# A third value buffer, a body for up to 192 tokens and a table made by GpSimd, in a kernel of sparse attention and routed experts

## The chip, the cores and the metric

The kernel runs on one core of a Trainium2 chip. Its time is the device time of one execution in microseconds (us), as the median of several runs. An execution was also recorded by the hardware profiler; every row below is from that record. The engines are PE (TensorE, matrix products; PEld is its loading of the stationary operand), DVE (VectorE), ACT (ScalarE), POOL (GpSimd) and SP (SyncE, which here issues nearly all loads).

## The reference

Attention over 24 blocks of 32 tokens, of which each block sees its neighbours, the first and last block and three blocks drawn at random; its output goes through a mixture of eight experts, one expert per token:

```python
# q, k, v: 4 batches x 8 heads x 768 tokens x 64
mask = |blk_i - blk_j| <= 1 or blk_i, blk_j in (first, last) or blk_j in sampled_blocks[blk_i]
attn = softmax(where(mask, q k^T / 8, -1e9)) v
x = attn as 3072 tokens x 512
logits = x @ w_gate + modality_bias[modality_id]      # 8 experts
e = argmax(logits);  p = softmax(logits)[e]
out[token] = p * (relu(x @ w1[e]) @ w2[e])            # 512 -> 1024 -> 512
```

Counted from the inputs, three experts get tokens: 1498, 442 and 1132. In groups of 256 that is five whole groups and 218 tokens, one and 186, four and 108.

## The kernel before, in words

**Attention.** The first and last block (which see everything) are worked densely. The other 22 blocks are taken two at a time and two batches at a time: 22 tiles `g` = 0..21, eleven for each half of the batches. A tile's keys lie in one of two `kbuf`, its values in one of two `vbuf`. Its value loads are `fetch_v` (L505, two block loads of 128 KB, L510) and `fetch_own` (L544, six, L549); two further blocks come from the tile before by copies of GpSimd in `share_v` (L527, L532). Products with the shared blocks are `weigh_shared` (L608), with the tile's own blocks `weigh_own` (L617). `turned` (L624) and `gate` (L634) then turn the output and work out the logits, and `put_row` writes the rows to `x_d` (L1316). The order on each engine is written out by hand: a clock of steps `t`, a table of lags, and `side(t, ...)`, which hangs a load on a step. Value loads hang on `last(g - 2)`, the step of the last scores of the tile that had the same buffer. SP issues its queue in program order, so a load that waits for its buffer holds up all behind it.

**Routing.** `finish` (L1175) makes from the counts of tokens per expert two tables. `hoh` (L1212), multiplied on PE (L1243), gives for every place in every group the number of its token (`gi`, L1081). `grp` (L1239) gives each group's expert, and in columns 22 and 23 the number of whole groups and of all. Two groups of full size are picked before all tokens are known (`NEAR` = 2) and worked into the tail of the attention.

**Experts.** A group has 256 tokens (`GT`). `gather` (L770) fetches its rows by an indirect DMA of GpSimd, `turn_blocks` or `turn_low` (L801) turns them. A weight is split into a rounded high part (ACT, L756) and a low rest (DVE, L759; for the four numbers in `POOL_SPLITS` GpSimd), and each product is three: high by high, high by low, low by high. `first_layer` has `up` (L810; L814, L815, L816: 32 times, weights stationary, 256 token columns moving) and `relu` (L818). `second_layer` has `down` (L824; L829, L830, L831: for each of eight feature blocks and both halves of the tokens, 512 columns of weights moving). `give` (L843) scales by `p` and scatters (L850). Groups 2 to 11 run in a loop without conditions; then `later(12)` asks at run time whether there is another group and whether it is a whole one or holds at most 128 tokens, which `half_group` (L1018) works with tokens as the stationary side. With these inputs there are twelve whole groups and one half group.

Of the kernel before, what the change touches and what calls it, by code (L numbers as in the profile page):

```python
# [30 lines left out]
GT = 256  # L31
NG = NTOK // GT
# [45 lines left out]
LATER = 19  # L78
XD = (7, 7)
# [12 lines left out]
def attention_moe(ctx, tc, kD, qD, qH, v0, v1, blocks, modality, w_gate, bias, w1, w2, out):  # L92
# [32 lines left out]
    with ExitStack() as actx:  # L125
# [18 lines left out]
        vbuf = [slot(7 + n)[:, 0:3072].rearrange("p (c f) -> p c f", c=3) for n in range(2)]  # L144
# [360 lines left out]
        def fetch_v(m, half):  # L505
            i, g = 2 * m + 1, half * NM + m
            vg = vbuf[g % 2]

            def rows_in(r, c, j):
                nc.sync.dma_start(vg[r, c, :].rearrange("p (b f) -> p b f", b=HB), vblock(half, j))  # L510

            if m < 2:
                for n, j in ((0, 0), (1, NB - 1)):
                    rows_in(slice(32 + 32 * n, 64 + 32 * n), 1, j)
            if m == 0:
                for n in range(2):
                    rows_in(slice(0, 32), 1 + n, i + 2 * n)
                for n in range(2):
                    rows_in(slice(96, P), n, i - 1 + 2 * n)
                return  # L520
            rows_in(slice(0, 32), 2, i + 2)
            rows_in(slice(96, P), 1, i + 1)
# [4 lines left out]
        def share_v(m, half):  # L527
            g = half * NM + m
            shared.append(g)
            new, old = vbuf[g % 2], vbuf[(g - 1) % 2]  # L530
# [13 lines left out]
        def fetch_own(m, half, n):  # L544
            i, g = 2 * m + 1, half * NM + m
            vg = vbuf[g % 2]
# [56 lines left out]
        def weigh_shared(g, o, a):  # L603
            vg = vbuf[g % 2]
# [6 lines left out]
        def weigh_own(g, o, a):  # L611
            vg = vbuf[g % 2]
# [197 lines left out]
        def up(g, c, f, o):  # L810
            h, l = wh[(8 * g + c) % NRING], wl[(8 * g + c) % NRING]
            o = o[:, (f % 2) * GT:(f % 2 + 1) * GT]
            fs = slice(f * P, (f + 1) * P)
            nc.tensor.matmul(o, lhsT=h[:, fs], rhs=xh[g % 2][:, c, :], start=c == 0 and f % 2 == 0, stop=False)  # L814
            nc.tensor.matmul(o, lhsT=h[:, fs], rhs=xl[g % 2][:, c, :], start=False, stop=False)  # L815
            nc.tensor.matmul(o, lhsT=l[:, fs], rhs=xh[g % 2][:, c, :], start=False, stop=c == 3 and f % 2 == 1)  # L816

        def relu(k, o):  # L818
            rh = hh[0][:, 2 * k:2 * k + 2, :].rearrange("p a b -> p (a b)")
            rl = hl[k // 2][:, k % 2 * 2:k % 2 * 2 + 2, :].rearrange("p a b -> p (a b)")  # L820
# [3 lines left out]
        def down(g, f, t, o):  # L824
# [6 lines left out]
            nc.tensor.matmul(o, lhsT=hl[f // 4][:, f % 4, ts_], rhs=h[:, fs], start=False, stop=f == 7)  # L831

# [10 lines left out]
        def give(g, t, o):  # L843
# [3 lines left out]
            else:  # L847
                nc.vector.tensor_scalar(og[t], o, w, None, ALU.mult)
            ix = si_e[g] if g < NEAR else si[:, 2 * g:2 * g + 2]
# [131 lines left out]
        def first_layer(g):  # L981
            for c in range(4):
                ahead(8 * g + c)
                if c == 0 and g + 1 < NGMAX:
                    if g == NEAR:
                        gather(g + 1)
                    if g == NG - 1:
# [4 lines left out]
                for f in range(8):  # L992
                    up(g, c, f, hp[f // 2])
            for k in range(4):
                relu(k, hp[k])

        def second_layer(g):
            for k in range(4):
                ahead(8 * g + 4 + k)
                for f in (2 * k, 2 * k + 1):  # L1000
                    for t in range(2):
                        down(g, f, t, op[t])
                if k == 1 and g + 1 < NGMAX:
# [3 lines left out]
            for t in range(2):  # L1007
                give(g, t, op[t])

# [8 lines left out]
        def half_group(g):  # L1018
# [34 lines left out]
            split(8 * g + 6, nc.gpsimd)  # L1053
# [120 lines left out]

        def finish():  # L1175
# [3 lines left out]
            nc.vector.tensor_tensor(gcount2, cnt, narrow, ALU.add)  # L1179
            yield  # L1180
# [3 lines left out]
            nc.vector.tensor_scalar(gwide, gcount2, 8, None, ALU.logical_shift_right)  # L1184
            yield
            gh = small.tile([P, E], F32, name="gh", bufs=1)
            nc.vector.tensor_tensor(gh, gnum, gwide, ALU.subtract)
            yield
            nc.vector.scalar_tensor_tensor(gh, gh, 16.0, iota_f[:, 0:E], ALU.mult, ALU.add)
# [5 lines left out]
            nc.vector.tensor_tensor(start[:, :, 0:E], before_e, gnum.unsqueeze(1).broadcast_to([P, E, E]), ALU.mult)  # L1195
            yield
            gbase = small.tile([P, E], F32, name="gbase", bufs=1)
# [3 lines left out]
            nc.vector.tensor_reduce(gfrom, start[:, :, 0:E], axis=AX.X, op=ALU.add)  # L1201
            hb = small.tile([P, NT, E], F32, name="hb", bufs=1)
# [6 lines left out]
            nc.vector.scalar_tensor_tensor(hc, hs, 2.0, rhi, ALU.mult, ALU.add)  # L1209
            yield  # L1210
# [4 lines left out]
            gend = small.tile([P, E], F32, name="gend", bufs=1)  # L1215
            nc.vector.tensor_scalar(gfrom, gfrom, float(NEAR), None, ALU.add)
            yield
            nc.vector.tensor_tensor(gend, gfrom, gnum, ALU.add)
            ge = work.tile([P, 512], F32, name="y", bufs=3)[:, 0:24 * E].rearrange("p (t e) -> p t e", e=E)
            gl = work.tile([P, 512], F32, name="y", bufs=3)[:, 0:24 * E].rearrange("p (t e) -> p t e", e=E)  # L1220
            i24 = iota_f[:, 0:24].unsqueeze(2).broadcast_to([P, 24, E])
            nc.vector.tensor_tensor(ge, gfrom.unsqueeze(1).broadcast_to([P, 24, E]), i24, ALU.is_le)
            yield
            nc.vector.tensor_tensor(gl, gend.unsqueeze(1).broadcast_to([P, 24, E]), i24, ALU.is_gt)
            yield
            nc.vector.tensor_tensor(ge, ge, gl, ALU.mult)
            yield
            nc.vector.tensor_tensor(ge, ge, iota_f[:, 0:E].unsqueeze(1).broadcast_to([P, 24, E]), ALU.mult)
            yield
            nc.vector.tensor_reduce(grp_f, ge, axis=AX.X, op=ALU.add)  # L1230
            nc.vector.tensor_reduce(grp_f[:, 23:24], gend, axis=AX.X, op=ALU.max)
            gw = small.tile([P, 1], F32, name="gw", bufs=1)
            nc.vector.tensor_reduce(gw, gh, axis=AX.X, op=ALU.max)
            yield
            nc.vector.tensor_scalar(gw, gw, 16.0, None, ALU.is_ge)
            yield
            nc.vector.tensor_tensor(grp_f[:, 22:23], grp_f[:, 23:24], gw, ALU.subtract)
            yield
            nc.vector.tensor_copy(grp, grp_f)  # L1239
# [98 lines left out]
        for g in range(2 * NM):  # L1338
# [11 lines left out]
            vt = last(g - 2) + VL[0]  # L1350
# [6 lines left out]
            for n in range(2):  # L1357
                side(last(g - 2) + VG[n][0], vg[n], VG[n][1])
# [110 lines left out]
        LOOP = MAN - {ET.PE}  # L1469
        with tc.manual_schedule(engines=LOOP):  # L1470
            for g in range(NEAR, NG):
                first_layer(g)
                second_layer(g)
        total = nc.values_load(grp[0:1, 23:24], min_val=NG, max_val=NGMAX, skip_runtime_bounds_check_because=NO_CHECK)
        wide = nc.values_load(grp[0:1, 22:23], min_val=NG - 1, max_val=NGMAX, skip_runtime_bounds_check_because=NO_CHECK)

        def later(g):
            if g == NGMAX:
                return
            with tc.If(total > g):  # L1480
                experts.clear()
                with tc.If(wide <= g) as less:
                    half_group(g)
                with less.Else():
                    experts.clear()
                    with tc.manual_schedule(engines=LOOP):
                        first_layer(g)
                        second_layer(g)
                    later(g + 1)

        later(NG)
# [36 lines left out]
```

## Time and profile before

| | us |
|---|---|
| median of three runs | 521.59 |
| the three runs | 517.51, 521.59, 521.68 |
| the profiled execution | 523.39 |
| its span, first to last instruction | 521.7 |
| mean granted clock of TensorE | 0.991 of full speed |
| busy: PE, PEld, DVE, ACT, POOL | 500.2, 422.4, 373.3, 335.4, 246.0 |

Busy time is summed over the whole span; the stages have different limits. Attention with the first two expert groups runs to about 252 us, the loop of groups to 502.4, the half group and the last stores to the end. The granted clock is a share of full speed: 1.00 is 2.4 GHz, 0.50 is 1.2 GHz.

### The profile page before, as it was taken

What the parts mean: (1) busy time and instruction counts of PE and PEld (TensorE: products, weight loads), DVE (VectorE), ACT (ScalarE), POOL (GpSimd) and SP (SyncE); (2) the same over time, 40 slices, a digit from 0 to 9 for tenths busy, and PEclk for the clock granted to TensorE, in tenths of its full rate; (3) what the DMA queues carried; (4) which work ended last, traced back from release to release, by engine and by line L of the source; (5) the groups of instructions that cost most, each with busy time, mean ns of one, the idle gap of its engine ahead of it and who ended that gap; (6) DMA issues with size and microseconds to landing.
All of it is one profiled execution on the core that took longest, in us unless ns stands there. A gap on an engine that the chain in (4) does not pass through costs nothing.

```text
span 521.7 us, 18917 instructions
## 1 busy us (share of the span) xinstructions
PE 500.2 (96%) x7124; PEld 422.4 (81%) x7124; DVE 373.3 (72%) x1069; ACT 335.4 (64%) x765; POOL 246.0 (47%) x517
## 2 busy tenths in 40 slices
PE   7999999979999998799999999999999999999994
PEld 5678677757878786698989798998989899898974
DVE  6886577676787888467985867667686766768572
ACT  4799887978879897544445655555564545655561
POOL 6788685566568882323175042322325222342422
PEclk9999999999999999989999999999999999999999
DMA  8977898798667769847788797879678686877950
GB/s 299 317 214 205 243 266 244 207 257 247 202 187 194 220 203 257 248 133 253 230 291 299 248 288 257 281 213 297 199 248 283 221 296 202 283 219 258 287 181 24
DMA packets 65143, 123.84 MB, mean 237 GB/s; under 512 B 9745, under 2 KB 17682, under 8 KB 65042
## 3 DMA queue, kind: packets, MB, share of 16 engines
q1 hardware_dynamic: 60784, 108.88, 68.7%
q0 software_dynamic: 4256, 13.65, 7.4%
q8 instruction: 58, 0.95, 0.8%
q14 instruction: 43, 0.35, 0.3%
q10 hardware_dynamic: 2, 0.00, 0.0%
HBM read 105.97 MB, written 12.86 MB: 228 GB/s over the span
## 4 chain that ended last, share of the span: by engine, by line
PE 77%; DMA 11%; DVE 5%; ACT 2%; issue 2%; SPq 1%; POOL 0%; ACTq 0%; POOLq 0%; DVEq 0%
PE bank L586 8%; PE bank L561 8%; PE bank L814 7%; PE bank L815 7%; PE bank L816 7%; PE bank L831 6%; PE bank L830 6%; PE bank L829 6%; DMA slot<-x_d,gi 5%; PE bank L608 4%; PE bank L617 4%; DMA slot<-w 3%; PE bank L634 3%; PE bank L448 2%; PE bank L430 2%
## 5 line engine op out<-in xcount | busy, mean ns | idle before, releaser
L759 DVE TENSOR_TENSOR slot<-slot 128x1024 fp32r<-128x1024 f32 x99 | 124.8, 1273 | 66.4 <-ACT slot L756 59.6
L756 ACT CAST slot<-slot 128x1024 fp32r<-128x1024 f32 x104 | 107.2, 1047 | 73.2 <-PE bank L815 47.8
L814 PE MATMUL bank<-slot 128*128 128x256 f32 x384 | 108.5, 283 | 0.0
L816 PE MATMUL bank<-slot 128*128 128x256 f32 x384 | 107.8, 281 | 0.0
L815 PE MATMUL bank<-slot 128*128 128x256 f32 x384 | 107.6, 280 | 0.0
L577 ACT ACTIVATE a<-y,mn 128x256 f32<-128x256 f32 x176 | 88.6, 510 | 5.5 <-DVE mn L569 5.5
L850 POOL DMA_INDIRECT out<-slot,si x20 | 27.3, 1363 | 104.5 <-ACT slot L846 101.4
L831 PE MATMUL bank<-slot 128*128 128x512 f32 x192 | 75.9, 396 | 0.5 <-DVE slot L822 0.5
L830 PE MATMUL bank<-slot 128*128 128x512 f32 x192 | 76.0, 396 | 0.0
L829 PE MATMUL bank<-slot 128*128 128x512 f32 x192 | 75.8, 395 | 0.0
L814 PEld LDWEIGHTS bank<-slot 128*128 128x128 f32 x384 | 72.4, 188 | 0.7 <-issue 0.2
L815 PEld LDWEIGHTS bank<-slot 128*128 128x128 f32 x384 | 72.2, 188 | 0.4
L816 PEld LDWEIGHTS bank<-slot 128*128 128x128 f32 x384 | 72.2, 188 | 0.0
L569 DVE CUSTOM_DVE_ANT_1 y<-bank,smask 128x256 f32<-128x256 f32 x176 | 66.2, 416 | 0.4 <-PE bank L561 0.2
L498 POOL COPY slot<-slot 128x128 f32 x264 | 63.5, 293 | 0.0
L591 ACT COPY at<-bank 128x512 f32<-128x512 f32 x88 | 50.6, 576 | 10.3 <-PE bank L586 10.1
L532 POOL TENSOR_SCALAR slot<-slot 32x1024 f32<-32x1024 f32 x40 | 41.6, 1040 | 32.4 <-DMA slot<-v 11.2
L586 PE MATMUL bank<-ident,a 128*128 128x128 f32 x352 | 52.0, 280 | 3.1 <-DVE lhs L387 2.7
L561 PE MATMUL bank<-slot,q_raw 64*32 64x256 f32 x1408 | 48.6, 382 | 0.3 <-issue 0.3
L586 PEld LDWEIGHTS bank<-ident,a 128*128 128x128 f32 x352 | 38.1, 141 | 7.1 <-issue 2.8
L831 PEld LDWEIGHTS bank<-slot 128*128 128x128 f32 x192 | 36.1, 188 | 9.5 <-DVE slot L822 0.9
L830 PEld LDWEIGHTS bank<-slot 128*128 128x128 f32 x192 | 36.0, 188 | 8.2 <-DVE slot L759 0.3
(302 smaller groups left out, 846.4 us busy)
## 6 DMA issues: line engine op xcount, KB each, us to landing
slot<-w SPq DMA_DIRECT2D x100, 512.0 KB
slot<-v SPq DMA_DIRECT2D x188, 128.0 KB
x_d<-xr SPq DMA_DIRECT2D x22, 256.5 KB
q_raw<-qH SPq DMA_DIRECT2D x22, 256.0 KB
slot<-slot SPq DMA_DIRECT2D x120, 32.0 KB
slot<-kD SPq DMA_DIRECT2D x13, 256.0 KB
slot<-v SPq DMA_DIRECT2D x4, 768.0 KB
slot<-v SPq DMA_DIRECT2D x12, 256.0 KB
```

The costliest lines, as they stand in the source:

```text
L561: nc.tensor.matmul(sp[u][32 * pr:32 * pr + 32, b * 256:(b + 1) * 256], lhsT=q[r, b * NPAIR + pr, n, :], rhs=kv[r, s0:s0 + 8, b, pr, :], st ...
L569: nc.vector.tensor_tensor_reduce(y[:, u, :].rearrange("p (s f) -> p s f", s=8), sp[u][:, b * 256:(b + 1) * 256].rearrange("p (s f) -> p s ...
L577: nc.scalar.activation(a[:, u, :], y[:, u, :], AF.Exp, bias=mn[:, u:u + 1], scale=-1.0, accum_out=total[:, u:u + 1])
L586: nc.tensor.transpose(tp[:, k:k + P], a[:, u, c * P:(c + 1) * P], ident)
L756: nc.scalar.copy(h, s)
L759: (eng or (nc.gpsimd if n in POOL_SPLITS else nc.vector)).tensor_tensor(l, s, h.bitcast(F32), ALU.subtract)
L814: nc.tensor.matmul(o, lhsT=h[:, fs], rhs=xh[g % 2][:, c, :], start=c == 0 and f % 2 == 0, stop=False)
L815: nc.tensor.matmul(o, lhsT=h[:, fs], rhs=xl[g % 2][:, c, :], start=False, stop=False)
L816: nc.tensor.matmul(o, lhsT=l[:, fs], rhs=xh[g % 2][:, c, :], start=False, stop=c == 3 and f % 2 == 1)
L829: nc.tensor.matmul(o, lhsT=hh[0][:, f, ts_], rhs=h[:, fs], start=f == 0, stop=False)
L830: nc.tensor.matmul(o, lhsT=hh[0][:, f, ts_], rhs=l[:, fs], start=False, stop=False)
L831: nc.tensor.matmul(o, lhsT=hl[f // 4][:, f % 4, ts_], rhs=h[:, fs], start=False, stop=f == 7)
```

## The change: what it does

1. **Values.** From tile 13 on there are three value buffers; the third lies in `slot(0)`. The value loads of these tiles hang on `last(g - 3)`, one tile sooner. Tile 13, the first in the new buffer, also loads the first and last block into it (two block loads more).
2. **A body for up to 192 tokens**, `group(g, False)`. `up` moves 192 columns. The first 128 tokens go through `down` as before; the remaining 64 through `down_both`, in which the stationary operand holds the high part of 64 tokens beside their low part, so that a feature block takes two matmuls and not three. `give_both` adds the two halves. It stands at group 11, and behind it the half group.
3. **Order and table.** `finish` puts one expert's rest of at most 192 tokens, then one of at most 128, behind the whole groups. `grp` is now made by GpSimd (33 rows of its queue); `hc`, from which `gi` comes, takes three more DVE operations, one of which reads `by` from GpSimd.
4. The half group's third split goes from GpSimd to DVE. The loop without conditions ends one group sooner, and its drain with it.

```diff
+        def vb(g):
+            if g < THIRD_FROM:                                   # 13
+                return vbuf[g % 2]
+            if len(vbuf) == 2:
+                vbuf.append(values_in(0))
+            return vbuf[(2, THIRD_FROM % 2, 1 - THIRD_FROM % 2)[(g - THIRD_FROM) % 3]]
...
-            if m < 2:
+            if m < 2 or g == THIRD_FROM:
                 for n, j in ((0, 0), (1, NB - 1)):
                     rows_in(slice(32 + 32 * n, 64 + 32 * n), 1, j)
...
-            vt = last(g - 2) + VL[0]
+            free = last(g - (3 if g >= THIRD_FROM else 2))
+            vt = free + VL[0]
...
-                side(last(g - 2) + VG[n][0], vg[n], VG[n][1])
+                side(free + VG[n][0], vg[n], VG[n][1])
...
+            nc.tensor.matmul(o, lhsT=h[:, fs], rhs=xh[g % 2][:, c, 0:n], start=c == 0 and f % 2 == 0, stop=False)
+            nc.tensor.matmul(o, lhsT=h[:, fs], rhs=xl[g % 2][:, c, 0:n], start=False, stop=False)
+            nc.tensor.matmul(o, lhsT=l[:, fs], rhs=xh[g % 2][:, c, 0:n], start=False, stop=c == 3 and f % 2 == 1)
...
+                nc.scalar.activation(rh, o, AF.Relu)
+                for r, to in ((slice(0, P), rl[:, :, 0:P]), (slice(P, n), hh[0][:, 2 * k:2 * k + 2, n:GT])):
+                    nc.vector.scalar_tensor_tensor(to, o[:, :, r], 0.0, rh[:, :, r].bitcast(F32), ALU.max, ALU.subtract)
...
+        def down_both(g, f, o):
+            h, l = wh[(8 * g + 4 + f // 2) % NRING], wl[(8 * g + 4 + f // 2) % NRING]
+            fs = slice((f % 2) * 512, (f % 2 + 1) * 512)
+            high = lambda: nc.tensor.matmul(o, lhsT=hh[0][:, f, P:GT], rhs=h[:, fs], start=f == 0, stop=f == 7)
+            low = lambda: nc.tensor.matmul(o[0:64], lhsT=hh[0][:, f, P:THREE], rhs=l[:, fs], start=False, stop=False)
+            for product in (high, low) if f < 4 else (low, high):
+                product()
+
+        def give_both(g, o):
+            nc.vector.tensor_copy(og[1][0:64], o[64:128])
+            nc.vector.tensor_tensor(og[1][0:64], o[0:64], og[1][0:64], ALU.add)
+            nc.vector.tensor_scalar(og[1][0:64], og[1][0:64], share[0:64, 2 * (g % 2) + 1:2 * (g % 2) + 2], None, ALU.mult)
+            scatter(g, 1)
...
-            split(8 * g + 6, nc.gpsimd)
+            split(8 * g + 6)
...
+            nc.vector.tensor_tensor(start[:, :, 0:E], before_e, inner.unsqueeze(1).broadcast_to([P, E, E]), ALU.mult)
...
+            nc.gpsimd.tensor_tensor(whole_n, inner, part[:, 0, :], ALU.add)
...
+            nc.gpsimd.tensor_scalar(by[:, 0:1], move[:, 0, 0:1], 2.0, float(2 * NEAR - 1), ALU.mult, ALU.add)
+            nc.gpsimd.tensor_scalar(by[:, 1:2], move[:, 1, 0:1], 2.0, 0.0, ALU.mult, ALU.add)
...
+            gp.tensor_copy(grp[:, 0:20], grp_f[:, 0:20])
+            gp.tensor_copy(grp[:, 21:24], grp_f[:, 21:24])
...
+            nc.vector.tensor_scalar(hs, rhi, by[:, 0:1], by[:, 1:2], ALU.is_ge, ALU.mult)
+            nc.vector.scalar_tensor_tensor(hs, code_of, pick[:, 0:1], hs, ALU.is_equal, ALU.mult)
+            nc.vector.tensor_tensor(hc, hc, hs, ALU.add)
...
-            nc.vector.tensor_tensor(ge, gfrom.unsqueeze(1).broadcast_to([P, 24, E]), i24, ALU.is_le)
...
-            nc.vector.tensor_copy(grp, grp_f)
...
-            for g in range(NEAR, NG):
+            for g in range(NEAR, NG - 1):
                 first_layer(g)
                 second_layer(g)
...
+        def whole(g):
+            with tc.If(narrower <= g) as less:
+                group(g, False)
+                if g + 1 < NGMAX:
+                    with tc.If(total > g + 1):
+                        half(g + 1)
+            with less.Else():
+                group(g)
+                later(g + 1)
```

SP's queue at the end of the attention; `slot<-v` are value loads, `slot<-w` weights, `x_d<-xr` rows written. Before, from the write of tile 19's rows on:

```order
L1316 DMA x_d<-xr 128x513
L510 DMA slot<-v 32x2x512 x2
L549 ISA
L549 DMA slot<-v 32x2x512
L549 ISA
L549 DMA slot<-v 32x2x512
...
L549 ISA
L549 DMA slot<-v 32x2x512
L745 ISA
L745 DMA slot<-w 128x512
L1316 DMA x_d<-xr 128x513
```

With the change, from the same write on:

```order
L1399 DMA x_d<-xr 128x513
L756 ISA
L756 DMA slot<-w 128x512
L1399 DMA x_d<-xr 128x513
L756 ISA
L756 DMA slot<-w 128x512
```

The eight value loads of the last tile have gone from here to one write of rows earlier; the weights follow the write directly.

GpSimd's queue at the end of the routing; `out<-slot,si_e` are scatters of the first early group, `slot<-x_d,gi` the gathers of groups 2 and 3. Before:

```order
L387 TENSOR_SCALAR lhs<-iota_f,rlo,code 128x128 x2
L759 TENSOR_TENSOR slot<-slot 128x1024
L850 DMA out<-slot,si_e_84 3072x512 x2
L770 DMA slot<-x_d,gi 128x513 x4
L759 TENSOR_TENSOR slot<-slot 128x1024 x2
```

With the change:

```order
L770 TENSOR_TENSOR slot<-slot 128x1024
L1256 TENSOR_TENSOR whole_n<-inner,part 128x8
...
L1276 TENSOR_TENSOR y<-iota_f,ends 128x192 x2
L1278 TENSOR_SCALAR y<-y 128x384
...
L1296 TENSOR_TENSOR grp_f<-y,gx 128x20
L1297 CAST grp<-grp_f 128x20
L1298 CAST grp<-grp_f 128x3
L886 DMA out<-slot,si_e_84 3072x512 x2
L781 DMA slot<-x_d,gi 128x513 x4
L770 TENSOR_TENSOR slot<-slot 128x1024 x2
```

All 33 rows of the table stand between the split and the scatters, and so ahead of the gathers.

DVE's queue in the half group, before (`L759` is a weight's low part, `L1037` the low part of the hidden values that PE multiplies next):

```order
L1022 TENSOR_SCALAR si_half<-si 128x1 x2
L759 TENSOR_TENSOR slot<-slot 128x1024 x2
L1037 TENSOR_TENSOR slot<-bank,slot 128x4x128
L759 TENSOR_TENSOR slot<-slot 128x1024
L1037 TENSOR_TENSOR slot<-bank,slot 128x4x128
```

With the change:

```order
L1062 TENSOR_SCALAR si_half<-si 128x1 x2
L770 TENSOR_TENSOR slot<-slot 128x1024 x3
L1077 TENSOR_TENSOR slot<-bank,slot 128x4x128
L770 TENSOR_TENSOR slot<-slot 128x1024
L1077 TENSOR_TENSOR slot<-bank,slot 128x4x128
```

One more low part of a weight stands ahead of the first low part of the hidden values.

## Rows read from the trace of the kernel before

**Rows 1.** Stretches: length; busy PE, PEld, DVE, ACT, POOL; clock, DMA share, GB/s.

```profile
150.00:180.00 30.00, 30.00 (x852) 23.63 (x846) 23.19 (x117) 27.24 (x91) 23.58 (x68) 1.00 0.72 203
...
217.20:219.90 2.70, 0.06 (x3) 0.00 (x0) 0.00 (x0) 0.00 (x0) 0.00 (x0) 0.86 0.96 352
219.90:226.00 6.10, 6.08 (x102) 5.47 (x102) 3.14 (x10) 3.61 (x6) 0.00 (x0) 0.50 0.27 99
...
480.00:502.40 22.40, 22.40 (x145) 20.34 (x144) 15.77 (x19) 12.21 (x16) 7.35 (x8) 1.00 0.80 249
```

**Rows 2.** Chain of waits at the attention's end: start, us, what.

```profile
209.13 0.94 PE bank L586 x8
...
217.26 2.65 issue
```

**Rows 3.** SP's timeline there: start, us until issued, line, transfer, count.

```profile
210.79 3.43 SPq L549 DMA_DIRECT2D slot<-v  x6
```

**Rows 4.** PE's timeline: the bounds of one group's two layers.

```profile
434.98 0.28 PE L814 MATMUL bank<-slot 128*128 128x256 f32 x1
...
446.25 0.40 PE L829 MATMUL bank<-slot 128*128 128x512 f32 x1
...
457.39 0.28 PE L814 MATMUL bank<-slot 128*128 128x256 f32 x1
```

**Rows 5.** Weight loads by form: count, busy us, mean ns, idle before.

```profile
L814 PEld LDWEIGHTS bank<-slot 128*128 128x128 f32 x384 | 72.4, 188 | 0.7 <-issue 0.2
...
L617 PEld LDWEIGHTS bank<-slot,at 128*32 128x32 f32 x1408 | 22.1, 113 | 0.5 <-issue 0.3
```

**Rows 6.** DVE's timeline in the half group, in brackets the idle time before.

```profile
507.05 1.23 DVE L759 TENSOR_TENSOR slot<-slot 128x1024 fp32r<-128x1024 f32 x1 [1.68 <-PE bank L1033]
508.49 0.69 DVE L1037 TENSOR_TENSOR slot<-bank,slot 128x512 fp32r<-128x512 f32 x1 [0.21 <-ACT slot L1036]
```

**Rows 7.** GpSimd operations by form, from the start of the program.

```profile
L292 POOL TENSOR_SCALAR t<-t 128x24 f32<-128x24 f32 x3 | 1.0, 319 | 0.3
...
L288 POOL TENSOR_TENSOR t<-rb 128x24 f32<-128x24 f32 x3 | 0.7, 233 | 0.2
...
L280 POOL TENSOR_TENSOR rm<-rm,t 128x72 f32<-128x72 f32 x1 | 0.3, 336 | 0.1
```

**Rows 8.** DVE's timeline at the end of the routing.

```profile
245.62 2.33 DVE L1187 TENSOR_TENSOR gh<-gnum,gwide 128x8 f32<-128x8 int32 x1
...
250.08 0.22 DVE L1195 TENSOR_TENSOR start<-before_e,gnum 128x64 f32<-128x64 f32 x1
...
252.79 1.22 DVE L759 TENSOR_TENSOR slot<-slot 128x1024 fp32r<-128x1024 f32 x1
...
257.80 4.63 DVE L759 TENSOR_TENSOR slot<-slot 128x1024 fp32r<-128x1024 f32 x4
```

**Rows 9.** GpSimd's timeline at the end of the routing.

```profile
245.54 2.39 POOL L759 TENSOR_TENSOR slot<-slot 128x1024 fp32r<-128x1024 f32 x1
254.17 1.09 POOL L850 DMA_INDIRECT out<-slot,si_e  x1 [6.24 <-DVE gfrom L1216]
...
263.32 1.73 POOL L770 DMA_INDIRECT slot<-x_d,gi  x1 [6.09 <-DMA slot<-w]
265.35 0.97 POOL L770 DMA_INDIRECT slot<-x_d,gi  x1 [0.30 <-issue]
```

**Rows 10.** The gathers from 262 to 276, us from issue to landing.

```profile
DMA to landing us min/median/max: 6.8/7.4/7.5
```

**Rows 11.** PE's timeline, first turn of group 2's rows.

```profile
272.96 0.60 PE L801 MATMUL bank<-ident,slot 128*128 128x128 f32 x4
```

**Rows 12.** Copies of GpSimd in the loop: ns least, median, most of all 40.

```profile
L779 POOL COPY slot<-slot x40: 387/393/1485, 283.1 to 489.2; 32x256 f32<-32x256 f32 x40
```

**Rows 13.** GpSimd's timeline, three of these copies in one row.

```profile
331.24 2.35 POOL L779 COPY slot<-slot 32x256 f32<-32x256 f32 x3 [4.92 <-DMA out<-slot,si]
```

**Rows 14.** DVE's timeline at the same time.

```profile
332.11 1.22 DVE L759 TENSOR_TENSOR slot<-slot 128x1024 fp32r<-128x1024 f32 x1 [1.66 <-ACT slot L756]
```

More of the change, by code (lines that the diff above doesn't have):

```diff
@@ L31 @@
 GT = 256
+THREE = 192
 NG = NTOK // GT
@@ L78 @@
 LATER = 19
+THIRD_FROM = 13
 XD = (7, 7)
@@ L529, in share_v @@
             shared.append(g)
-            new, old = vbuf[g % 2], vbuf[(g - 1) % 2]
+            new, old = vb(g), vb(g - 1)
             for r, c in ((slice(96, P), 0), (slice(0, 32), 1)):
@@ L992, in first_layer, with second_layer @@
                 for f in range(8):
-                    up(g, c, f, hp[f // 2])
+                    up(g, c, f, hp[f // 2], GT if wide_ else THREE)
             for k in range(4):
-                relu(k, hp[k])
-        def second_layer(g):
+                relu(k, hp[k], GT if wide_ else THREE)
+        def second_layer(g, wide_=True):
             for k in range(4):
@@ L1000, in second_layer @@
                 for f in (2 * k, 2 * k + 1):
-                    for t in range(2):
+                    for t in range(2 if wide_ else 1):
                         down(g, f, t, op[t])
+                    if not wide_:
+                        down_both(g, f, op[1])
                 if k == 1 and g + 1 < NGMAX:
@@ L1006, in second_layer @@
                         gather(g + 2)
-            for t in range(2):
+            for t in range(2 if wide_ else 1):
                 give(g, t, op[t])
+            if not wide_:
+                give_both(g, op[1])
         def down_part(g, f, n, o):
@@ L1173, in choose, with folded @@
                 yield
+        def folded(ap):
+            for n in (4, 2, 1):
+                nc.gpsimd.tensor_tensor(ap[:, :, 0:n], ap[:, :, 0:n], ap[:, :, n:2 * n], ALU.add)
         def finish():
@@ L1179, in finish @@
             nc.vector.tensor_tensor(gcount2, cnt, narrow, ALU.add)
+            gcount3 = small.tile([P, E], I32, name="gcount3", bufs=1)
+            nc.vector.tensor_scalar(gcount3, gcount2, -64.0, None, ALU.add)
             yield
@@ L1469, in attention_moe, with group, half @@
         LOOP = MAN - {ET.PE}
+        def group(g, wide_=True):
+            experts.clear()
+            with tc.manual_schedule(engines=LOOP):
+                first_layer(g, wide_)
+                second_layer(g, wide_)
+        def half(g):
+            experts.clear()
+            half_group(g)
         with tc.manual_schedule(engines=LOOP):
-            for g in range(NEAR, NG):
+            for g in range(NEAR, NG - 1):
                 first_layer(g)
                 second_layer(g)
-        total = nc.values_load(grp[0:1, 23:24], min_val=NG, max_val=NGMAX, skip_runtime_bounds_check_because=NO_CHECK)
-        wide = nc.values_load(grp[0:1, 22:23], min_val=NG - 1, max_val=NGMAX, skip_runtime_bounds_check_because=NO_CHECK)
+        load = lambda n, least, most: nc.values_load(grp[0:1, n:n + 1], min_val=least, max_val=most, skip_runtime_bounds_check_because=NO_CHECK)
+        total, wide, narrower = load(23, NG, NGMAX), load(22, NG - 1, NGMAX), load(21, NG - 1, NGMAX + 64)
+        def whole(g):
[7 more added lines that the diff above has]
+                later(g + 1)
         def later(g):
@@ L1480, in later @@
             with tc.If(total > g):
-                experts.clear()
                 with tc.If(wide <= g) as less:
-                    half_group(g)
+                    half(g)
                 with less.Else():
[L1485 to L1491, printed above, removed]
+                    whole(g)
+        whole(NG - 1)
 _SHAPE_OUT = (NTOK, HD)
```

103 lines of the change are left out of this document (69 added, 34 removed).

## The prediction, made before the changed kernel was run

> **What bounds the kernel now.** I read the table of busy time first: PE is busy for 500 of 521.7 us, so an edit counts where PE works less or waits less. Then the stretches [rows 1]: in the middle of the attention PE is busy 30.00 of 30 us and in the loop of groups 22.40 of 22.4, both at the 2.4 GHz level (clock 1.00). There, moving other engines' work changes nothing. Two stretches differ. From 217.2 to 219.9 PE is busy 0.06 of 2.70 us, no other engine works, and the DMA share is 0.96 with 352 GB/s. From 219.9 to 226.0 PE is busy again but at clock 0.50, the 1.2 GHz level. The chain of waits puts the gap down to issue, 2.65 us, in the middle of a run of matmuls [rows 2]: no instruction of another engine is named as its releaser. Last I read the timelines: SP's for the transfers ahead of the gap, PE's for the pitch of its matmuls, DVE's and GpSimd's for the end of the routing.
>
> The profiled execution took 523.39 us, 1.8 over the median of 521.59; one run of the three took 517.51. The sum below stands against 523.39.
>
> **Part 1, the values.** From tile 13 on, nine tiles' loads of eight transfers (128 KB each) are issued one tile sooner, and two transfers are added at tile 13; on SP they pass the writes of rows and the loads of `q`, which are issued behind them now. In the middle that costs nothing: PE is covered there, 30.00 of 30 [rows 1]. If that cover were gone, the two added transfers would cost what two of the six at the end take to issue, 2/6 of 3.43 = 1.1 us [rows 3]. At the end, the last tile's eight transfers (1 MB) go from just ahead of the gap. The last was issued by 214.22 [rows 3], three microseconds before PE stopped, and with the weights behind them they keep the DMA at 0.96 through the gap [rows 1]. I take the gap to be PE's own instructions coming late behind this traffic, since nothing else released it. With a megabyte less it probably goes. Worth: 2.64 us idle and, at half clock, half of 6.10 = 3.05: **-5.7**. Ends: 0 if the weights, issued sooner now, fill the DMA as much, and -5.7.
>
> **Part 2, the body for 192 tokens.** It takes the place of one of twelve whole groups: the counts 218, 186 and 108 put exactly one rest at 186.
> Down: a whole group has 48 matmuls between 446.25 and 457.39, 0.232 each [rows 4]. The new body has 8 x 3 + 8 x 2 = 40: 8 x 0.232 = **-1.9**.
> Up: 96 matmuls between 434.98 and 446.25, 0.1174 each for 256 columns [rows 4]. With 192 columns they take 0.088 if the columns decide, which would be -2.8. But each also loads 128 columns of weights. Loads of 128 columns take 188 ns and of 32 columns 113 ns [rows 5], 0.78 ns a column, so 0.100 for 128. The transposes, 128 columns loaded for 128 moved, go at 0.94 / 8 = 0.1175 [rows 2]. That bounds the gain from the other side at nothing. I take 0.105, beside the load's slope: 96 x 0.0125 = **-1.2** (ends -2.8 and 0).
> The Trainium skill speaks against the width here: "TensorE: Matmul & The Clock Gate", section "LDWEIGHTS (loading the stationary operand)", gives a weight load its columns over 1.2 in ns, 107 for 128, whatever moves. By it the term would be -1.0, by the columns alone -2.8; the trace's slope is nearer to the page.
> The relu's low part becomes two narrower DVE operations per block and `give_both` three of 64 rows; DVE is busy 15.77 of 22.40 in such a stretch [rows 1], so PE hides them. The three values read for the branch stand on PE's queue where two stood; the branch of before shows no gap in front of the half group, so 0 to one late fetch of instructions, 2.65 as in [rows 2]; I take 0. The drain and the shorter loop: 0, GpSimd is busy 7.35 of 22.40 [rows 1].
>
> **Part 3, the half group.** The third split now runs on DVE ahead of the first low part of the hidden values. DVE ends the second split at 508.28 and the low part starts at 508.49 [rows 6]; with one more split of 1.23 between, it starts at 509.5, and PE, which multiplies it next, waits **+0.9** (0 to 1.0).
>
> **Part 4, the table by GpSimd.** DVE loses thirteen operations and gains some eleven small ones: about even. GpSimd gains 34 operations in a chain. Sixteen narrow ones with two inputs and two casts at 0.233, nine with a scalar at 0.319; by the step from 24 to 72 columns, 0.103 for 48 [rows 7], four of 192 columns at 0.59, two folds at 0.39 and 0.28, and one of 384 at about 1.1. That is 11.2; with 0.07 between two (0.2 idle before three [rows 7]) 13.6, less somewhat, as most are narrower than the priced ones: 13. It starts when DVE has `inner`, as at 250.08 now or a little before [rows 8], say 249.7, and ends at 262.7. Behind it in the queue stand two scatters (1.09 each with the pause [rows 9], 2.2) and then the gathers of group 2: 264.9 in place of 263.32 [rows 9]. The second gather of the group was issued at 265.35 and landed 7.4 later [rows 10], at 272.75; PE turned these rows at 272.96 [rows 11]. The slack is 0.2, so PE would wait 1.4. One DVE operation of this chain waits for `by`, the ninth of the 34; behind it stand the places of the tokens and four splits, with what the removed operations free as room.
>
> But GpSimd does not run freely beside DVE. A copy that takes 0.393 took up to 1.485 [rows 12]: three of them took 2.35 [rows 13] while DVE subtracted a weight's low part from 332.11 for 1.22 [rows 14]. The other way round, a DVE operation on 8 columns took 2.33 [rows 8] while GpSimd's split of 2.39 ran [rows 9]. Where both have two inputs in memory, one waits for the whole of the other. In the chain's 13 us DVE has one such split at 252.79 and four at 257.80 [rows 8], of which at least four fall in: 4 x 1.16 = 4.6. The gathers come at 269.5, 6.2 later than now, and PE waits 6.0. After a wait of 2.65 the clock cost 3.05 more [rows 1]; here 0 to 3.05, I take 1.5. Together **+7.5**. Ends: 1.4 and 12.5 (below). SP reads the table before it loads group 2's weights, which PE needs after the turn; they come late in the shadow of the same wait.
> The Trainium skill has this as a lock in "SBUF — State Buffer", section "Who interferes with whom": whoever of the two starts first holds a shared pair of ports for its whole instruction. The trace agrees (1.485 for 0.393); by the rule without exception the whole exclusion below holds, an estimate of 528.0.
>
> **The sum.** 523.4 - 5.7 - 1.9 - 1.2 + 0.9 + 7.5 = **523.0**. The median of before is 521.6: within 1%, which is 5.2 us and about what a measurement of this kernel can tell from no change.
>
> **The rivals.**
> *The chain stays hidden* (0.25). GpSimd slips its short operations in between DVE's; PE waits 1.4 and keeps its clock: 523.0 - 6.1 = 516.9, and 515.3 with `up` at the columns' rate. For it: most of the 34 are short, and DVE has small operations between its splits. Against: every long collision in the trace made the other wait.
> *Whole exclusion, slower* (0.18). Each two-input operation of DVE holds GpSimd up and each of GpSimd's holds DVE up: beside four splits a fifth, the 912-column compare and the short ones, about 8 us in place of 4.6. Then the table is ready near 270.7, the gathers go at 272.9 and PE waits 9.4, with 3.05 of half clock 12.5, 5.0 more than my term: 528.0. It decides once the gathers are issued later than about 268, from where the wait eats what parts 1 and 2 give.
> *The gap at 217 stays* (0.16). The weights are issued sooner and fill the DMA in the same way. Against the median then: 521.6 - 1.9 - 1.2 + 0.9 + 7.5 = 526.9; with the chain hidden 520.8.
> *Narrow matmuls are slow* (0.06). No matmul of this rounded type with under 256 columns is in the trace. At the transposes' time per column, 0.1175 / 128 = 0.92 ns, 192 take 0.176: 96 x (0.176 - 0.105) = +6.8: 529.8.
> *The new body is not taken* (0.02): parts 2's -3.1 falls away, 526.1.
>
> **How the numbers follow.** My forecast has 0.28, other mishaps and gains 0.05. The likeliest case's own range is 520.5 to 526, by the ends of the clock's and up's terms. Under 516.4 lie half of the hidden chain and a little of the rest: faster by over 1% 0.20. Over 526.8 lie most of the whole exclusion, half of the case in which the gap stays, and the slow matmuls: 0.27. The rest, 0.53, is within 1%. For eight in ten the range reaches into the hidden chain and to the whole exclusion: 515.5 to 529.
>
> **What would show it.** Up's rows of 192 columns: a pitch of 0.105, or 0.088, or 0.176. 16 rows of `down_both` at 0.232. Between 216 and 226 no gap of PE and a clock of 1.00. GpSimd's 33 rows from 249.7: operations far longer than 0.23 to 0.32 beside DVE's splits, the end of the casts, the issue of the first gather (264.9, 269.5 or 272.9), and PE's idle time in front of the first turn of group 2. In the half group PE's wait for the hidden values' low part. The forecast is wrong if the gathers go before 265 or after 272, or if the gap at 217 is still there.

## The result: slower by 1.4%, and the profile after

| | before | with the change |
|---|---|---|
| median of six runs, us | 520.72 | 527.58 |
| the runs | 517.51 to 523.39 | 526.99 to 529.59 |
| ratio, 95% interval | 1 | 1.0138 (1.0105 to 1.0172) |
| span of the profiled execution | 521.7 | 525.1 |

Where the time went, from the starts of the same matmuls in PE's two timelines (us):

| piece of the program | before | after | difference |
|---|---|---|---|
| start to the first matmul of group 1 | 252.43 | 249.35 | -3.1 |
| group 1 to group 2 | 24.19 | 33.27 | **+9.1** |
| group 2 to group 3 | 23.30 | 22.52 | -0.8 |
| group 3 to the group that has the new body | 180.03 | 179.93 | -0.1 |
| that group (256 columns before, 192 after) | 22.49 | 20.01 | **-2.5** |
| half group, first to last matmul | 12.44 | 13.52 | **+1.1** |
| last matmul to the end | 6.8 | 6.5 | -0.3 |

Groups are counted from 0. The first two end at 276.6 in the kernel before, not at 252 as its description has it; at 252 the second of them begins.

The page: PE is as busy as before, GpSimd 19 us more, with 33 instructions more.

```profile
PE 500.1 (95%) x7116; PEld 420.5 (80%) x7116; DVE 376.0 (72%) x1075; ACT 334.6 (64%) x765; POOL 265.2 (51%) x550
```

**The table.** GpSimd's timeline at the end of the routing, against [rows 9]:

```profile
247.41 0.20 POOL L1256 TENSOR_TENSOR whole_n<-inner,part 128x8 f32<-128x8 f32 x1 [2.51 <-DVE si_e L1150]
...
255.22 1.92 POOL L1217 TENSOR_TENSOR y<-y 128x96 f32<-128x96 f32 x3
257.09 1.17 POOL L1284 TENSOR_SCALAR all_n<-inner 128x8 f32<-128x8 f32 x1
258.35 2.45 POOL L1217 TENSOR_TENSOR all_n<-all_n 128x4 f32<-128x4 f32 x3
260.76 1.30 POOL L1287 TENSOR_SCALAR has<-pick 128x2 f32<-128x2 f32 x1
262.14 0.19 POOL L1288 TENSOR_SCALAR has<-has 128x1 f32<-128x1 f32 x1
...
264.60 0.21 POOL L1298 CAST grp<-grp_f 128x3 int32<-128x3 f32 x1
265.29 1.12 POOL L886 DMA_INDIRECT out<-slot,si_e  x1 [0.48 <-ACT slot L767]
...
268.00 1.01 POOL L781 DMA_INDIRECT slot<-x_d,gi  x1 [0.30 <-issue]
```

The chain runs from 247.41 to 264.81, 17.4 us. An operation on a single column takes 0.19 at 262.14; one on eight columns takes 0.20 at 247.41; between 257 and 262 operations on eight and on two columns take 1.17 and 1.30. What ran on DVE then, against [rows 8]:

```profile
252.32 1.52 DVE L770 TENSOR_TENSOR slot<-slot 128x1024 fp32r<-128x1024 f32 x1
...
255.73 4.75 DVE L770 TENSOR_TENSOR slot<-slot 128x1024 fp32r<-128x1024 f32 x4
...
260.62 0.20 DVE L1121 TENSOR_TENSOR gi<-bank,to 128x38 int32<-128x38 f32 x1
260.73 1.22 DVE L770 TENSOR_TENSOR slot<-slot 128x1024 fp32r<-128x1024 f32 x1
```

The four splits from 255.73 on take 4.75, against 4.63 without the chain: DVE loses a tenth of a us on them, and GpSimd gets about one operation in between two splits. DVE is held up too: the split at 252.32 takes 1.52 in place of 1.22, beside GpSimd's operation on 384 columns (2.47, from 251.30), and three new operations for `hc` stand ahead of it; PE waits 1.25 for it in group 1. The tokens' places (`gi`) are there at 260.8. In the kernel before the first gather followed them by 0.3 us, at 263.32:

```profile
262.85 0.20 DVE L1081 TENSOR_TENSOR gi<-bank,to 128x38 int32<-128x38 f32 x1
```

Now the gathers stand behind the chain and go at 268.0. PE's timeline, against [rows 11], and the clock around it (columns as in [rows 1]):

```profile
253.90 0.39 PE L827 MATMUL bank<-slot 128*128 128x256 f32 x1 [1.25 <-DVE slot L770]
...
271.17 0.40 PE L850 MATMUL bank<-slot 128*128 128x512 f32 x1
276.00 0.47 PE L812 MATMUL bank<-ident,slot 128*128 128x128 f32 x1 [4.43 <-DMA slot<-x_d,gi]
276.97 0.90 PE L812 MATMUL bank<-ident,slot 128*128 128x128 f32 x3 [0.51 <-DMA slot<-x_d,gi]
...
278.95 0.63 PE L848 MATMUL bank<-slot 128*128 128x512 f32 x1
```

```profile
271.20:277.00 5.80, 0.87 (x4) 0.21 (x2) 3.44 (x1) 1.04 (x1) 5.47 (x4) 0.79 1.01 401
277.00:281.30 4.30, 4.30 (x14) 3.61 (x15) 3.53 (x4) 1.53 (x2) 0.50 (x1) 0.50 0.83 283
```

PE waits 4.9 us for the gathers, and then works 4.3 us at the 1.2 GHz level, which costs half of them, 2.15. With the 1.25 in group 1 this makes 8.3 of the 9.1.

**The gap at 217** is down to 0.50 us, and the stretch 219.90 to 226.00 now has clock 1.00. What is left stands at the same place of the program: the last tile has 32 products with the shared blocks, and PE stops among them, before the change after the 15th:

```profile
219.91 1.13 PE L608 MATMUL bank<-slot,at 128*64 128x64 f32 x17 [2.65 <-issue]
```

With the change it stops after the 17th:

```profile
218.76 0.68 PE L619 MATMUL bank<-slot,at 128*64 128x64 f32 x15 [0.50 <-issue]
```

```profile
219.90:226.00 6.10, 5.93 (x122) 5.32 (x120) 5.08 (x15) 3.56 (x6) 0.00 (x0) 1.00 0.34 101
```

PE has a longer gap in the attention, 55 us sooner, and the clock of the 15 us after it is 0.89:

```profile
164.38 1.04 PE L619 MATMUL bank<-slot,at 128*64 128x64 f32 x29 [1.39 <-issue]
```

**The new body.** Its first matmul, its first `down` and the half group's first, against [rows 4]:

```profile
485.07 0.25 PE L825 MATMUL bank<-slot 128*128 128x192 f32 x1
...
495.76 0.41 PE L848 MATMUL bank<-slot 128*128 128x512 f32 x1
...
505.08 0.39 PE L1067 MATMUL bank<-slot 128*128 128x512 f32 x1
```

Up: 10.69 / 96 = 0.111 a matmul, against 0.117 with 256 columns. Down: 9.32 / 40 = 0.233, as before, eight fewer.

**The half group** on DVE, against [rows 6]:

```profile
507.05 0.69 DVE L861 COPY slot<-bank 64x512 f32<-64x512 f32 x1
507.78 0.68 DVE L862 TENSOR_TENSOR slot<-bank,slot 64x512 f32<-64x512 f32 x1
508.50 0.48 DVE L863 TENSOR_SCALAR slot<-slot,share 64x512 f32<-64x512 f32 x1
508.90 0.20 DVE L1062 TENSOR_SCALAR si_half<-si 128x1 int32<-128x1 int32 x2
509.02 3.48 DVE L770 TENSOR_TENSOR slot<-slot 128x1024 fp32r<-128x1024 f32 x3
512.43 0.68 DVE L1077 TENSOR_TENSOR slot<-bank,slot 128x512 fp32r<-128x512 f32 x1
```

Not only the third split stands ahead of the hidden values' low part. The three operations of `give_both` hold DVE until 508.98, so that the first split starts 3.9 us after the half group's first matmul; before, it started 1.7 after it. PE waits 0.71 us there for ACT's relu, in front of two transposes that now stand sooner in its queue, and 0.17 for DVE's low part; before the change it had no wait in the half group:

```profile
512.55 0.44 PE L1073 MATMUL bank<-ident,slot 128*128 128x128 f32 x2 [0.71 <-ACT slot L1092]
513.16 0.51 PE L1056 MATMUL bank<-slot 128*128 128x256 f32 x2 [0.17 <-DVE slot L1077]
```

### The profile page after: what moved, and what is told of

Its sections match the earlier page's. It is cut to its first block, busy times and chain, and to the rows that moved or that the text cites. A ratio compares the mean times of both kernels' runs of the same rounds, so it can differ in the third digit from the quotient of the medians.

```text
span 525.1 us, 18946 instructions
## 1 busy us (share of the span) xinstructions
PE 500.1 (95%) x7116; PEld 420.5 (80%) x7116; DVE 376.0 (72%) x1075; ACT 334.6 (64%) x765; POOL 265.2 (51%) x550
## 4 chain that ended last, share of the span: by engine, by line
PE 34%; DMA 11%; DVE 3%; SPq 3%; issue 3%; POOL 1%; ACT 1%; POOLq 0%; DVEq 0%
DMA out<-slot,si 7%; PE bank L825 6%; PE bank L827 6%; PE bank L826 6%; PE bank L850 5%; PE bank L849 5%; PE bank L848 5%; DMA slot<-x_d,gi 3%; SPq L792 2%; DMA slot<-slot 1%; DVE slot L770 1%; DMA slot<-w 1%; POOL slot L781 1%; DVE gmost L1232 0%; SPq L759 0%
## 5 line engine op out<-in xcount | busy, mean ns | idle before, releaser
L827 PE MATMUL bank<-slot 128*128 128x256 f32 (+1 forms) x384 | 107.8, 281 | 1.4 <-DVE slot L770 1.4
L825 PE MATMUL bank<-slot 128*128 128x256 f32 (+1 forms) x384 | 108.3, 282 | 0.0
L826 PE MATMUL bank<-slot 128*128 128x256 f32 (+1 forms) x384 | 107.6, 280 | 0.0
L886 POOL DMA_INDIRECT out<-slot,si x20 | 29.4, 1472 | 96.8 <-ACT slot L879 82.8
L827 PEld LDWEIGHTS bank<-slot 128*128 128x128 f32 x384 | 72.4, 188 | 1.8 <-DVE slot L770 1.8
L848 PE MATMUL bank<-slot 128*128 128x512 f32 x184 | 73.4, 399 | 0.0
L849 PE MATMUL bank<-slot 128*128 128x512 f32 x184 | 73.3, 398 | 0.0
L850 PE MATMUL bank<-slot 128*128 128x512 f32 x184 | 73.2, 398 | 0.0
L825 PEld LDWEIGHTS bank<-slot 128*128 128x128 f32 x384 | 72.4, 189 | 0.6
L826 PEld LDWEIGHTS bank<-slot 128*128 128x128 f32 x384 | 72.3, 188 | 0.4
L597 PE MATMUL bank<-ident,a 128*128 128x128 f32 x352 | 53.1, 283 | 1.1 <-ACT a L431 0.5
L790 POOL COPY slot<-slot 32x256 f32<-32x256 f32 x40 | 19.6, 490 | 46.5 <-DMA out<-slot,si 34.7
L850 PEld LDWEIGHTS bank<-slot 128*128 128x128 f32 x184 | 34.9, 190 | 8.3 <-DVE slot L841 0.2
```

The costliest lines, as they stand in the source:

```text
L597: nc.tensor.transpose(tp[:, k:k + P], a[:, u, c * P:(c + 1) * P], ident)
L825: nc.tensor.matmul(o, lhsT=h[:, fs], rhs=xh[g % 2][:, c, 0:n], start=c == 0 and f % 2 == 0, stop=False)
L826: nc.tensor.matmul(o, lhsT=h[:, fs], rhs=xl[g % 2][:, c, 0:n], start=False, stop=False)
L827: nc.tensor.matmul(o, lhsT=l[:, fs], rhs=xh[g % 2][:, c, 0:n], start=False, stop=c == 3 and f % 2 == 1)
L848: nc.tensor.matmul(o, lhsT=hh[0][:, f, ts_], rhs=h[:, fs], start=f == 0, stop=False)
L849: nc.tensor.matmul(o, lhsT=hh[0][:, f, ts_], rhs=l[:, fs], start=False, stop=False)
```

## The experiments

The kernel before took 524.3 to 525.6 beside these (medians of 17 to 29 runs), so each is told as a ratio to it, with its 95% interval. Single profiles differ by several us in the attention, so a stage is read from its own first to its own last matmul.

**The table on DVE.** The same operations, `nc.gpsimd` replaced, the part behind `by` moved behind `hoh` and spread over the yields (places at which other work of the schedule comes in between).

```diff
-            gp = nc.gpsimd
+            gp = nc.vector
```

> The changed kernel with the same 34 operations on DVE: those of `by` where they stood, the table behind the places of the tokens, as before the change. Theory A (beside DVE's splits GpSimd's chain takes 17.4 us, and it stands ahead of the gathers of group 2, so PE waits before the first turn and loses clock, some 9 us in all): the first gather goes 1 to 4 us later than in the kernel before instead of following a chain of 17.4 us, PE's wait in front of the turn falls to 1 to 4 us, and the time from 527.6 to 520 to 523. Rival W (the table is too much work at that place on any engine): DVE, full there, passes on the same delay, 526 to 528. Rival V (the loss lies with the values or the new body): 527 to 528, whatever the wait before the turn does.

Ratio 1.0116 (1.0060 to 1.0172); from group 1 to group 2 29.8 us, so 3.5 of the 9.1 came back, not the 5 to 8 that theory A gave the whole time; rival W has the larger part. The first gather goes at 270.14, counted from group 1's first matmul 5.7 us later than before and not 1 to 4. PE's wait for the gathers is gone, and another stands in its place, in group 1:

```profile
258.54 0.39 PE L827 MATMUL bank<-slot 128*128 128x256 f32 x1 [1.72 <-DVE slot L770]
265.47 0.39 PE L827 MATMUL bank<-slot 128*128 128x256 f32 x1 [1.58 <-DVE slot L770]
```

DVE, full there, came to the four splits at 264.19, behind the table; from 260 to 266 the mean clock was 0.72. So the work costs at that place on either engine.

**The table given.** The lines that work the table out are removed; what is left out is named below.

```diff
+            for n0, n1, value in ((0, 20, 0), (6, 10, 7), (10, 12, 1), (12, 13, 7), (21, 22, 11), (22, 23, 12), (23, 24, 13)):
+                nc.gpsimd.memset(grp[:, n0:n1], value)
```

> The changed kernel with the table's values written as constants by seven small writes of GpSimd; only `by` is still worked out there (leaves out the working out of the table). From the first matmul of group 1 to the first of group 2 took 24.2 us before, 33.3 with the change, 29.8 with all of the table on DVE. Theory A (the loss is the table's work wherever it stands ahead of something full: GpSimd's gathers or DVE's splits): 24.5 to 26.5, and the time against the kernel before between -2 and +1.5 us (the new body -2.4, the half group +1.1). Rival B (the loss comes from the DVE operations that were added for the order, and the wait for `by`): 29 or more, time +4 or more.

From group 1 to group 2 24.9 us: all but 0.7 of the 9.1 is the working out of the table, and rival B falls. The time came out above what was expected, 1.0042 (1.0010 to 1.0075), +2.2 us. In its profile everything from group 1 on is 0.4 us shorter than before. By that the rest would lie in the attention, where a single profile can't place it; this is argued, not shown.

**A longer chain.**

```diff
+            for _ in range(16):
+                gp.tensor_scalar(gx, gx, 1.0, 0.0, ALU.mult, ALU.add)
```

> The changed kernel with sixteen more narrow operations in GpSimd's chain (0.33 each with the pause, 5.3 us). Theory A: every us of the chain goes through to the gathers and to PE: from group 1 to group 2 38 to 39 us, time 5 us above the changed kernel's. Rival C (PE waits there for something else, weights or DVE, and the chain is hidden behind it): 33 to 35, time the same.

1.0225 (1.0172 to 1.0279), 4.5 us above the changed kernel; group 1 to group 2 37.6. The sixteen took 4.66, the gathers went after them and PE waited 8.9 in place of 4.9:

```profile
273.25 4.66 POOL L1297 TENSOR_SCALAR gx<-gx 128x20 f32<-128x20 f32 x16
...
281.85 1.01 POOL L781 DMA_INDIRECT slot<-x_d,gi  x1 [0.30 <-issue]
```

```profile
288.86 0.47 PE L812 MATMUL bank<-ident,slot 128*128 128x128 f32 x1 [8.19 <-DMA slot<-x_d,gi]
...
290.06 0.90 PE L812 MATMUL bank<-ident,slot 128*128 128x128 f32 x3 [0.72 <-DMA slot<-x_d,gi]
```

Of the 4.66 us, 4.0 came as PE's wait and 4.4 in the interval: nearly all of what is added to the chain goes through.

**A short table.** On DVE the old eight operations with `inner` for `gnum`; what only the last groups need (the half group's entry, the counts) behind the tokens' places.

```diff
+            nc.vector.tensor_reduce(grp_f, ge, axis=AX.X, op=ALU.add)
...
+            nc.vector.tensor_copy(grp, grp_f)
...
             yield from rows_of(tp, NCOL, gi, si, turned_low)
+            nc.vector.tensor_reduce(has[:, 3:4], gend, axis=AX.X, op=ALU.max)
...
+            nc.vector.tensor_copy(grp, grp_f)
```

> The changed kernel with `by` on GpSimd and the table on DVE in eight operations where before had thirteen; the half group's entry and the three counts follow after the tokens' places, behind the splits. Theory A: 25 to 27.5 us from group 1 to group 2, time against before -1.5 to +2. Rival B: 29 or more, +4 or more.

(Before the change the table took twelve operations, not thirteen.) Group 1 to group 2 25.8 us, as theory A has it; the ratio 1.0050 (1.0019 to 1.0081), +2.6, a little above. PE still waits twice for splits; DVE has more small operations ahead of them than before:

```profile
259.30 0.38 PE L827 MATMUL bank<-slot 128*128 128x256 f32 x1 [0.40 <-DVE slot L770]
...
263.83 0.39 PE L827 MATMUL bank<-slot 128*128 128x256 f32 x1 [0.72 <-DVE slot L770]
```

**The half group's third split back on GpSimd**, alone and with the short table:

```diff
-            split(8 * g + 6)
+            split(8 * g + 6, nc.gpsimd)
```

> The changed kernel with the half group's third split on GpSimd again. By the order of DVE's operations PE waits 0.9 to 1.3 us less in the half group: 526.3 to 526.7 against 527.6. If GpSimd's split was holding DVE up there by as much (the lock the other way): 527.5 to 528.

> The same with the half group's third split on GpSimd again, as before: half a us to 1 us less than the short table alone; against the kernel before -2.5 to +1.5 us. From the first matmul of the half group to PE's last: 12.9 us as before, where the changed kernel took 14.3.

Alone 1.0124 (1.0079 to 1.0168), with the short table 1.0049 (1.0012 to 1.0085): neither is told apart from its partner. In the latter's trace the half group takes 13.2 from first to last matmul, against 13.5 with the split on DVE and 12.4 before: 0.3 came back, not 0.5 to 1, and not the 0.9 to 1.3 of the first of the two. (By the starts of the matmuls the expectation's 12.9 and 14.3 are 12.4 and 13.5.) PE waits 0.17 for DVE's low part, and now also for GpSimd's split, as the trace of the former shows:

```profile
523.50 0.39 PE L1055 MATMUL bank<-slot 128*128 128x256 f32 x1 [0.36 <-POOL slot L770]
```

**The values.** Two buffers in the changed kernel (`THIRD_FROM = 99`), the values part alone in the kernel before, and two buffers with the short table:

> The changed kernel with two value buffers throughout, loads as before the change. If the last tile's loads cause the gap of PE near 217 us (theory G1), the gap and the half clock behind it come back: 527.6 + 3 to 5 = 531 to 533. If the gap of PE is an event that comes at one place or another whatever these loads do (G2; the changed kernel's own profile has one of 1.39 us near 164 with half clock behind it): 527 to 528. If the values part is the cause of the loss (rival V): 521 to 524.

> The kernel before with the third value buffer and the sooner loads alone. G1 (the loads cause the gap near 217): the gap goes, 516 to 518 against 520.7. G2 (the gap moves to another place): 520 to 521.5. Rival V (the sooner loads harm): 524 or more.

> The short table and the half group's third split on GpSimd, now with two value buffers as before the change: the new body without the values part and without the long chain. From the trace's pieces (table and turn +1.6, next group +0.4, body -2.5, half group +0.8) 0 against the kernel before: -2 to +2 us. If the values part costs something in the attention that single profiles can't show among PE's wandering gaps, this kernel is 1 to 2.5 us better than the same with three buffers (which stood at 1.0049 of before); if not, it stays at 1.003 to 1.006.

1.0107 (1.0054 to 1.0160), 0.9994 (0.9966 to 1.0022) and 1.0029 (0.9990 to 1.0067). The values alone change nothing; the 5.7 us of the forecast, 1.1%, lie outside that interval. Whether the third buffer costs a little in the other two can't be told: 1.0107 stands against 1.0138 with it, 1.0029 against 1.0049. In the profile of the values alone, PE's gap is back at its place, after the 17th of the 32 products. The last of the tile's loads was issued at 212.67, 9.5 us before PE stopped and not 3.0, and within the gap the DMA share is 0.48, against 0.96 in [rows 1]:

```profile
224.61 1.12 PE L618 MATMUL bank<-slot,at 128*64 128x64 f32 x15 [2.42 <-issue]
```

```profile
222.20:224.60 2.40, 0.00 (x0) 0.00 (x0) 0.00 (x0) 0.00 (x0) 1.12 (x2) 0.77 0.48 129
```

With two buffers in the changed kernel a gap stands at this place too, and another far from these loads:

```profile
58.30 0.93 PE L597 MATMUL bank<-ident,a 128*128 128x128 f32 x7 [2.07 <-issue]
...
222.19 0.69 PE L619 MATMUL bank<-slot,at 128*64 128x64 f32 x17 [1.79 <-issue]
```

G1 falls. G2 is right in that the gap comes whatever these loads do, but the place does not wander: in ten of this case's twelve profiles PE stops at this same place, for 0.5 to 2.7 us, and what changes is how long. Over all twelve, from 30 to 230 us, PE has 44 gaps of at least 0.6 us that are put down to issue. They stand at only 15 places in the order of its matmuls (with three buffers the one of [rows 2] lies two matmuls later and counts once), and these are whole multiples of 126 matmuls apart, to within 5. In 41 of the 44, PE goes on 2.2 to 2.9 us after the start of a packet of 16 KB on the DMA queue q8, which carries instructions; of all moments about one in seven lies so. The kernel before has 58 of these packets, for 7124 matmuls with as many weight loads:

```profile
q8 instruction: 58, 0.95, 0.8%
```

At the gap of [rows 2] one starts between 217.1 and 217.2, as PE stops; in the profile of the values alone one starts between 222.1 and 222.2, again as PE stops:

```profile
q8 instruction: 1, 0.02, 89.3%
```

```profile
q8 instruction: 1, 0.02, 67.1%
```

So at these gaps PE had most likely run out of instructions, and the next block came late. The profile names no engine for a packet; that these are PE's is read from the places and the times. Why a block comes late in one execution and not in another no run shows. Other traffic is not ruled out: in the 7 us ahead of the gap of the values alone the DMA moved 301 GB/s. The value loads do not decide it: this place and the one 125 matmuls ahead of it cost 0.9 to 3.9 us together in the nine profiles with three buffers, and 1.9 to 2.7 in the three with two.

**The body not taken.**

```diff
-            gp.tensor_scalar(has[:, 1:2], has[:, 1:2], -64.0, 63.0, ALU.mult, ALU.add)
+            gp.tensor_scalar(has[:, 1:2], has[:, 1:2], 0.0, 63.0, ALU.mult, ALU.add)
```

> The changed kernel with the number in the table that chooses the body set so that the rest of 186 tokens goes through the whole group's body. If the new body is worth what its rows show (20.0 us in place of 22.4 from its first matmul to the half group's first): that interval is 22.4, and the time 1 to 2 us above the changed kernel's 1.0138, less what three operations of DVE in front of the half group cost: 1.015 to 1.018. If the narrow body gave nothing: no difference in the interval.

1.0204 (1.0155 to 1.0252), above what was expected, though the intervals of the two kernels overlap. The interval is the expected one, 22.6 to the half group's first matmul. Ahead of it, at the branch that is now taken, PE waits 0.6 us more; the profile names ACT's scaling of the group before:

```profile
490.75 0.39 PE L825 MATMUL bank<-slot 128*128 128x256 f32 x1 [0.58 <-ACT slot L879]
...
513.32 0.39 PE L1067 MATMUL bank<-slot 128*128 128x512 f32 x1
```

The half group then took 13.1: without `give_both` 0.7 of its 1.1 stays, with the third split. PE's one wait there is the 0.71 for ACT's relu.

No version beat the kernel before. With the body and the short table the pieces are -2.5 in the body, 0.8 to 1.1 more in the half group, 1.6 between groups 1 and 2, and between groups 2 and 3 0.9, 0.4 and, with two value buffers, 3.2 (24.2, 23.7 and 26.5 against 23.3). From group 1 to the end these three profiles are 1.0 longer, 0.25 shorter and 2.8 longer than that of the kernel before: no gain is left.

## Why the prediction came out as it did

The time lies 4.6 us over the forecast of 523.0. It is inside the range, 515.5 to 529, but over the 520.5 to 526 of the forecast's own case; it is inside because the range was drawn out to the whole exclusion, which did not come. That much is luck. From median to median the change lost 6.9 us, and the pieces from group 1 on give 6.5.

**The gap of the values part, -5.7: this step failed.** "PE's own instructions coming late" fits what the profiles show; that they come late behind these loads, and "with a megabyte less it probably goes", does not. The gap stands at a fixed place of PE's order with these loads ahead of it or without, for 0 to 2.7 us, and the values alone made no difference (0.9994). The profile of before had one of the longest at that place, and I took a loss of one execution for one that the change removes. The sign that I had named for it, no gap near 217 and a clock of 1.00, was nearly met in the changed kernel's profile and proved nothing. What came is in substance the rival "the gap stays", worked against the median: 526.9. With this term at nothing and the median of 520.7 the sum is 520.7 - 1.9 - 1.2 + 0.9 + 7.5 = 526.0.

**The chain by GpSimd, +7.5: the mechanism was right, the size a little small.** Measured 9.1 in front of group 2, of which 0.8 came back behind it. The chain's length was 17.4 (13 and 4.6 were forecast). The 268.0 of the first gather can't be held against the 269.5 as it stands, since the program was 3.1 us sooner there: counted from group 1's first matmul it went 7.8 us later than before, not 6.2. The wait for the gathers was 4.9 (6.0), the clock 2.15 (1.5); not foreseen was the wait of 1.25 for a split in group 1. "Whole exclusion" did not come: PE waited 4.9 and not 9.4. The Trainium skill's lock ("SBUF — State Buffer", "Who interferes with whom") would let either engine hold the other up. The trace shows both: beside DVE's row of splits GpSimd's short operations waited, up to 1.30, and DVE lost 0.12 on four; beside GpSimd's own long operations DVE waits, a split of 1.2 us for 5.02 while two splits of GpSimd run, 4.69 together (before the change 5.08):

```profile
273.56 5.02 DVE L770 TENSOR_TENSOR slot<-slot 128x1024 fp32r<-128x1024 f32 x1 [7.13 <-ACT slot L767]
```

"The chain stays hidden" fell; the longer chain shows that nothing covers what is added to it.

**The body, -3.1: -2.5.** Down came as worked out (0.233, eight fewer). Up was mis-sized: 0.111 a matmul and not 0.105, so -0.6 and not -1.2. It lies between the slope of the weight loads (0.100) and the transposes (0.1175), nearer to the latter. The Trainium skill's 107 ns for a load of 128 columns ("TensorE: Matmul & The Clock Gate", "LDWEIGHTS (loading the stationary operand)") was nearer than my 105. "Narrow matmuls are slow" and "not taken" fell.

**The half group, +0.9: 1.1**, but only part by the cause given. The third split without `give_both` made 0.7, and with the split back on GpSimd 0.8 stayed, with `give_both` ahead of the splits; I had put that down as hidden by the mean busy time of a whole group's stretch. PE was to wait for DVE's low part; it waited 0.17 for this and 0.71 for ACT's relu, as its queue has the transposes sooner.

## What to carry to other kernels

A gap that the chain puts down to issue is not won by taking away what stands ahead of it in time: compare several runs' times first, count the matmuls up to it in a second profile, and look among the DMA queues for packets of instructions. Work that is moved to an idle engine is only free if nothing urgent stands behind it in that engine's queue; here four gathers did. A chain of 34 tiny operations, 17.4 us long, made PE wait 4.9, with a stretch at half clock on top, and of 4.66 us more 4.0 went through to PE. An operation that is hidden in a long stretch by its share of busy time is not hidden at the stretch's end, where the next one's first inputs wait behind it.

## What the runs showed of the hardware

Beside DVE's splits of 1.2 us, GpSimd operations on two and eight columns took 1.17 to 1.30, where others on one and eight took 0.19 and 0.20; GpSimd got in about one operation per split, while four splits of DVE were lengthened from 4.63 to 4.75 in all. The other way round, one split of DVE took 5.02 beside two of GpSimd. Matmuls of the rounded type with 192 moving columns go at a pitch of 0.111 against 0.117 for 256: a quarter fewer columns, 5% less time. PE's gaps put down to issue between 30 and 230 us, 44 of at least 0.6 us in twelve profiles, stand at 15 places, whole multiples of 126 matmuls apart to within 5, and 41 of them end 2.2 to 2.9 us after a packet of 16 KB of instructions starts.
